# Attention jobs 4 to 7 beside the first half's feed-forward, and a different route for the second weight's decoding

## The chip, the core and the metric

The kernel is one program on one core of a Trainium2 chip. The metric is the device time of one execution in microseconds; lower is better. The profile is one profiled execution of the same program. A core has five engines that run side by side, each taking its own instructions strictly in order: TensorE (PE, matrix products; PEld are its weight loads), VectorE (DVE), ScalarE (ACT), GpSimd (POOL) and SyncE (SP), which here issues nearly all DMA transfers. Two more things matter below. A DMA that has to wait for its source or its buffer makes every later DMA of the same issuing engine wait too. And matrix results live in PSUM, here in eight tiles, which only VectorE and ScalarE read in this kernel.

## What is computed

Attention with a decay bias over 8 batches of 8 heads, 576 positions and 64 dimensions per head, and then a feed-forward layer on the result:

```python
scores = scale * np.matmul(q, k.transpose(0, 1, 3, 2))
s_pos = np.maximum(s, 0.0)
cum = np.cumsum(s_pos, axis=-1)
bias = -(cum[:, :, :, None] - cum[:, :, None, :])
scores = np.where(causal, -1000000000.0, scores + np.minimum(bias, 0.0))
scores = scores - np.max(scores, axis=-1, keepdims=True)
attn = np.exp(scores)
attn = attn / (np.sum(attn, axis=-1, keepdims=True) + 1e-09)
attn_out = np.matmul(attn, v)
x = attn_out.transpose(0, 2, 1, 3).reshape(B * S, H * D)   # 4608 x 512
h = x @ w_in                                               # 4608 x 2048
g = np.where(h >= 1, h, np.where(h <= -1, 0.0, (h + 1) ** 2 / 4))
return g @ w_out                                           # 4608 x 512
```

The two weights arrive as 64-bit floats, seen by the kernel as pairs of 32-bit integers.

## The kernel before

**Attention.** A job is one pair of heads of one batch, and one half of the queries: `hf` 0 has the first 320 positions, `hf` 1 the last 256. There are 64 jobs; the four pairs of batch 0 in the first half are jobs 0 to 3, the same pairs in the second half jobs 4 to 7. A job runs through eight slots (`att_slot`, from L468): its queries and keys are split into a leading and a remaining part (`att_prep`, L320), score blocks are computed on PE (L385, L386), VectorE adds the mask and takes the minimum (L391), ScalarE takes the exponential and its row sums (L402), the weights are scaled and split in two 16-bit halves on GpSimd, ScalarE and VectorE (`weights_t`, L408 to L429), and a transposing DMA (L430) brings them into the layout that the product with the values needs. Slot 7 of a job computes the product for the job before it (`att_out`, L437), and its result is scaled and split into the feed-forward's input `x` (L459, L460). `x0_0` is that input for batch 0, first half; `x0_1` the one for the second half.

**Feed-forward.** For each batch and half, 16 tiles `h` of 128 hidden units (12 matmuls each, L502) are turned into `g` by ScalarE (L514, L528), VectorE (L517, L518) and GpSimd (L529), and 16 times 12 matmuls with the second weight sum up four tiles `y` (L541). Two `h` tiles fit in PSUM.

**The weights.** Each weight is cut in 16 chunks of 128 x 512 values. For each, `decode` (L187) forms the 32-bit value from the two integers: ScalarE writes the absolute value of the high word (L193), VectorE clamps it from below and keeps the row maximum (L194), shifts (L195) and puts sign and low bits back (L201, or L203 and L204); in every second chunk ScalarE first prepares the low bits (L200). When all peaks of a weight (of half of it for `w2`) are known, `scale` (L206) makes one power of two from them: a maximum over the partitions through PE (`column_max`, L105; the tile is `row_wi`, `row_wo`), then spread to all partitions (`spread`, L113; `col_wi`, `col_wo`). `split` (L219) then writes the high 16-bit half on ScalarE (L222) and the low one, for 8 chunks of `w2` on VectorE (L230), for the other 8 on ScalarE and GpSimd (L227, L228). The first weight's names are `wir`, `WI`; the second's `wor` (as loaded), `WO` (decoded, then split).

**The order of the work.** First 1: jobs 0 to 3, with two chunks of the first weight decoded per pair of slots (L574 to L580), then its `scale` and `split`. Then the loop over `j` (L606): steps 0 to 15 each compute one `h` tile of batch 0, first half, and run two tasks of the second weight, of which there are 32; steps 16 to 31 compute the `y` matmuls of that half. Attention goes on from step `ATT_FROM` = 12, two slots a step, so 40 slots up to step 31. From step 32 on, each step does one slot and half an `h` or `y` step. The order in which instructions stand on each engine is not that of the source: a scheduler with priorities (`tc.high_priority`) sets it when the program is built.

**Buffers.** A chunk of the second weight is loaded into a buffer with tag `x0` or `x1`, two of each, in turn. The input `x` of the feed-forward uses the same tags, and `x0_0` occupies one of the `x0` while its `h` tiles are computed. So the even chunks have one buffer and the odd ones two. `load(c + 2)` (L596) follows `decode(c)`. Queries, keys and the scaled values (`vb`, L349) have a single buffer each, so that a job's preparation waits until the job before is through with them.

## Time and profile before

| | |
|---|---|
| median of 3 runs | 1178.55 us (1178.08 to 1179.56) |
| the profiled execution's own time | 1180.32 us |
| its span, first to last instruction | 1178.5 us |
| PE busy | 1013.1 us, 86% of the span |
| VectorE busy | 892.5 us, 76% |
| ScalarE busy | 746.2 us, 63% |
| GpSimd busy | 693.4 us, 59% |
| mean granted PE clock | 0.961 |

A row of a windows view gives a stretch of the span in us, and for each engine its busy time and number of instructions, then the granted PE clock, the busy share of the DMA engines and their GB/s. A row of a view by lines gives line, engine, operation, output and inputs, shapes and count, then busy time, mean ns of one, and after the second bar the idle time that stood ahead of these instructions with what ended it. A row of a timeline or of the chain gives the start in us, the duration in us, and the instruction. A row of the waits gives who waited for whom: us in total, times, longest.

### The profile page before, as it was taken

How to read it: one execution, taken by the hardware profiler on the slowest of the kernel's cores; microseconds unless marked ns; L12 is line 12 of the kernel's file. 1: busy time of each engine (PE TensorE's matmuls, PEld its weight loads, DVE VectorE, ACT ScalarE, POOL GpSimd, SP SyncE). 2: the span in 40 equal slices, each digit the busy share in tenths (PEclk: the TensorE clock that was granted, in tenths of full speed). 3: DMA queues.
4: the chain of work that ended last, by engine and by line, in shares of the span. 5: the costliest groups of instructions: out<-in, count | busy, mean ns of one | idle time of the engine just before them, and what ended most of it. 6: DMA issues, size and time to landing. Idle time of an engine off the chain costs nothing.

```text
span 1178.5 us, 25143 instructions
## 1 busy us (share of the span) xinstructions
PE 1013.1 (86%) x8470; PEld 780.1 (66%) x8470; DVE 892.5 (76%) x2403; ACT 746.2 (63%) x1719; POOL 693.4 (59%) x1169
## 2 busy tenths in 40 slices
PE   0234697599998999899999999899999999899998
PEld 0122364478776877687768877677777767687787
DVE  7878987778777877778777877787777767787633
ACT  4656587467757775677657775667566665677533
POOL 3865248676546765566556654766557554676522
PEclk9997898689999999999998999999999999899999
DMA  8895326667538763676539763876457643767300
GB/s 245 208 197 134 121 66 153 153 139 159 139 77 189 155 156 84 132 164 150 134 78 174 158 142 76 185 143 154 101 124 159 133 118 84 159 136 158 80 25 19
DMA packets 343082, 158.04 MB, mean 134 GB/s; under 512 B 291113, under 2 KB 324265, under 8 KB 342953
## 3 DMA queue, kind: packets, MB, share of 16 engines
q1 hardware_dynamic: 333248, 146.50, 56.3%
q10 hardware_dynamic: 9704, 9.93, 2.7%
q8 instruction: 67, 1.10, 0.4%
q14 instruction: 63, 0.51, 0.1%
HBM read 75.33 MB, written 9.73 MB: 72 GB/s over the span
## 4 chain that ended last, share of the span: by engine, by line
PE 57%; DVE 12%; POOL 11%; DMA 11%; issue 6%; ACT 4%; SPq 0%; DVEq 0%; ACTq 0%; POOLq 0%
PE y L541 24%; PE h L502 23%; DMA pt<-pb 4%; PE px L448 4%; DMA vt<-vb 3%; PE s L385 3%; PE s L386 2%; POOL pb L423 2%; POOL pb L426 2%; DVE pb L429 2%; DMA wor<-in_moe_w_out_dram 1%; POOL vb L351 1%; DVE p L391 1%; DMA wir<-in_moe_w_in_dram 1%; POOL pb L425 1%
## 5 line engine op out<-in xcount | busy, mean ns | idle before, releaser
L502 PE MATMUL h<-x,WI 128*128 128x256 f16 (+1 forms) x3072 | 452.9, 292 | 24.8 <-DVE u L518 16.9
L541 PE MATMUL y<-g,WO 128*128 128x256 f16 (+1 forms) x3072 | 452.3, 290 | 16.5 <-POOL g L529 9.9
L502 PEld LDWEIGHTS <-WI 128*128 128x128 f16 x3072 | 291.9, 100 | 119.6 <-issue 30.4
L541 PEld LDWEIGHTS <-WO 128*128 128x128 f16 x3072 | 287.6, 99 | 107.0 <-issue 24.5
L529 POOL TENSOR_TENSOR g<-u,g 128x320 f16<-128x320 f32 (+1 forms) x256 | 202.4, 790 | 205.8 <-ACT g L528 200.1
L514 ACT ACTIVATE u<-h,ub,us 128x320 f32<-128x320 f32 (+1 forms) x256 | 149.4, 584 | 168.2 <-PE h L502 160.1
L402 ACT ACTIVATE p<-p,mn 64x64 f32<-64x64 f32 (+4 forms) x320 | 178.7, 559 | 114.9 <-DVE mn L391 96.5
L517 DVE SCALAR_TENSOR_TENSOR h<-h,ws,u 128x320 f32<-128x320 f32 (+1 forms) x256 | 133.1, 520 | 107.6 <-ACT u L514 107.1
L423 POOL TENSOR_SCALAR pb<-p,rs 64x128 f16<-64x128 f32 (+4 forms) x160 | 112.8, 705 | 154.0 <-DVE rs L419 114.8
L385 PE MATMUL s<-K,Q 128*128 128x288 f32 (+4 forms) x384 | 150.6, 395 | 41.8 <-DVE mn L391 31.9
L429 DVE SCALAR_TENSOR_TENSOR pb<-p,rs,pb 64x128 f16<-64x128 f32 (+4 forms) x160 | 131.9, 825 | 51.0 <-POOL pb L423 50.3
L426 POOL TENSOR_TENSOR pb<-p,pb 64x128 f16<-64x128 f32 (+4 forms) x160 | 165.0, 1032 | 9.1
L391 DVE CUSTOM_DVE_ANT_0 p<-s,mask 64x64 f32<-64x64 f32 (+4 forms) x320 | 134.7, 422 | 46.8 <-PE s L386 40.7
L518 DVE SCALAR_TENSOR_TENSOR u<-u,r,h 128x320 f32<-128x320 f32 (+1 forms) x256 | 130.2, 510 | 8.7 <-DVE h L517 0.9
L424 ACT ACTIVATE p<-p,rs 64x64 f32<-64x64 f32 (+4 forms) x160 | 89.3, 559 | 66.2 <-DVE rs L419 63.4
L386 PE MATMUL s<-K,Q 68*128 68x288 f32 (+4 forms) x384 | 121.9, 319 | 8.9 <-ACT p L424 4.7
L448 PE MATMUL px<-pt,vt 128*64 128x256 f16 (+3 forms) x1536 | 92.1, 269 | 29.5 <-DMA pt<-pb 18.3
L385 PEld LDWEIGHTS s<-K,Q 128*128 128x128 f32 (+1 forms) x384 | 74.4, 194 | 64.4 <-DVE mn L391 40.4
L528 ACT CAST g<-u 128x320 f16<-128x320 f32 (+1 forms) x256 | 108.0, 422 | 13.9 <-DVE u L518 13.9
L448 PEld LDWEIGHTS <-vt 128*64 128x64 f16 x1536 | 76.8, 118 | 53.8 <-issue 27.3
L425 POOL TENSOR_SCALAR pb<-p 64x128 f16<-64x128 f32 (+4 forms) x160 | 91.2, 571 | 5.5 <-ACT p L424 2.4
L386 PEld LDWEIGHTS s<-K,Q 68*128 68x128 f32 (+1 forms) x384 | 75.6, 197 | 11.6 <-ACT p L424 5.1
(116 smaller groups left out, 961.9 us busy)
## 6 DMA issues: line engine op xcount, KB each, us to landing
rk<-in_k_dram SPq DMA_DIRECT2D x64, 288.0 KB
rq<-in_q_dram SPq DMA_DIRECT2D x64, 160.0 KB
rk<-in_k_dram SPq DMA_DIRECT2D x64, 160.0 KB
v<-in_v_dram SPq DMA_DIRECT2D x32, 288.0 KB
wir<-in_moe_w_in_dram SPq DMA_DIRECT2D x16, 512.0 KB
rq<-in_q_dram SPq DMA_DIRECT2D x64, 128.0 KB
wor<-in_moe_w_out_dram SPq DMA_DIRECT2D x16, 512.0 KB
out_dram<-o ACTq DMA_DIRECT2D x32, 160.0 KB
```

What stands on the lines that cost most here:

```text
L385: T.matmul(sc[:R, :c1 - c0], Q1[:, hd, qo:qo + R], K1[:, hd, c0:c1], start=True, stop=False)
L386: T.matmul(sc[:R, :c1 - c0], Q2[:KC, hd, qo:qo + R], K2[:KC, hd, c0:c1], start=False, stop=True)
L391: ttr[0] = V.tensor_tensor_reduce(out=Pt[:R, c0:c1], in0=sc[:R, :c1 - c0], in1=mask[:R, mo:mo + c1 - c0], scale=1.0, scalar=3.0e38 if mn i ...
L402: A.activation(Pt[:R, :W], Pt[:R, :W], AF.Exp, bias=m2[:R], scale=-1.0, accum_out=sums[n, i][:R, hd:hd + 1])
L423: G.tensor_scalar(his[0], pv, rs[:R, :1], 1.0, ALU.mult, ALU.mult)
L426: G.tensor_tensor(los[1], pw, his[1], ALU.subtract)
L429: V.scalar_tensor_tensor(los[0], pv, rs[:R, :1], his[0], ALU.mult, ALU.subtract)
L448: T.matmul(px[hd * D:(hd + 1) * D, lo:N], VT[:, vl * NB + j, hd * D:(hd + 1) * D], PT[:, 4 * j + 2 * hd + pl, lo:], start=(m == 0), stop=( ...
L502: T.matmul(h[:, :N], WI[4 * kt + ft // 4][:, wl, ft % 4 * P:(ft % 4 + 1) * P], x[:, kt, xl], start=(n == 0), stop=(n == 3 * NKT - 1),)
L514: first = A.activation(u, h[:, :N], AF.Relu, bias=ubi[b], scale=usc[b]).ins
L529: G.tensor_tensor(g[:, 1], u, g[:, 0], ALU.subtract)
L541: T.matmul(ys[b, hf, m][:, :N], WO[8 * (m // 2) + ft // 2][:, wl, c0:c0 + P], g[:, gl], start=(ft == 0 and n == 0), stop=(ft == NFT - 1 an ...
```

## The change

It has three parts.

1. **Attention in steps 0 to 31.** `ATT_FROM` goes. Steps 0 to 31 now do one slot each, and two in every fourth step: again 40 slots, so that step 32 finds the same job.
2. **The second weight's decoding and splitting.** The clamp moves from VectorE to GpSimd (new L195) and no longer delivers a row maximum. Instead, a new pass of ScalarE over the decoded chunk writes absolute values into the chunk's load buffer and adds them up by row (new L210). `scale` uses the largest row sum as the bound and leaves out two small VectorE steps. All 16 low halves now go over ScalarE and GpSimd (`POOL_LO`). The loads' buffers are now the two of tag `raw`, which the prefix sums used at the program's start, and those of `x0`, in the order raw, x0, raw; three chunks are loaded ahead, and `load(c + 3)` follows `decode(c)`.
3. **The value scales of batch 0** (`batch_scales_v(0)`, a second maximum over the partitions through PE) move from ahead of job 0 into its slot 6.

```diff
-POOL_LO = {'wi': (2, 3, 7, 11, 15), 'wo': range(1, 16, 2)}
+POOL_LO = {'wi': (2, 3, 7, 11, 15), 'wo': range(16)}
-ATT_FROM = 12
...
             A.activation(w, hw.bitcast(F32), AF.Abs)
-            V.tensor_scalar(w, w, LEAST_HI, LEAST_HI, ALU.max, ALU.max, accum_out=self.peak[:, c:c + 1])
+            if self.sums:
+                G.tensor_scalar(w, w, LEAST_HI, LEAST_HI, ALU.max, ALU.max)
+            else:
+                V.tensor_scalar(w, w, LEAST_HI, LEAST_HI, ALU.max, ALU.max, accum_out=self.peak[:, c:c + 1])
...
+            if self.sums:
+                A.activation(
+                    raw[:, :NC // 2].rearrange("p n t -> p (n t)").bitcast(F32), w, AF.Abs,
+                    accum_out=self.peak[:, c:c + 1],
+                )
...
-        WO[WO_LAG:], WO, (("x0", 2), ("x1", 2)), 2,
+        WO[WO_LAG:], WO, ((ap, "raw", 2), (gp, "x0", 2), (ap, "raw", 2)), 2, True,
...
     def batch_start(b):
         batch_v(b)
-        batch_scales_v(b)
+        if b:
+            batch_scales_v(b)
...
             att_slot(j, k)
+            if j == 0 and k == 6:
+                batch_scales_v(0)
...
-    for c in range(2):
+    for c in range(3):
         w2.load(c, w1.bound[0])
...
                 w2.decode(c)
-                w2.load(c + 2)
+                w2.load(c + 3)
...
-        for _ in range(1 if j >= 2 * NFT else 2 if j >= ATT_FROM else 0):
+        for _ in range(1 if j >= 2 * NFT else 1 + (j % 4 == 3)):
             att_slot(t // 8, t % 8)
```

How the instructions then stand, at three places. In a row, the name left of the arrow is what is written; a name's first numbers are its own (`s0_1_0_0` is a score block of pair 0, query block 1, head 0; `wor15` is chunk 15 of the second weight), its last number only counts tiles.

On PE, at the start of the program, before: the maximum of the value scales (`row_m0`, `col_m0`) stands ahead of job 0's score blocks.

```order
L108 MATMUL row_m0_183<-ident_77,mt0_180 1x128
L118 LDWEIGHTS ones_82
L118 MATMUL col_m0_189<-t16_m0_187,ones_82 128x1
L385 MATMUL s0_0_0_0_227<-K1_90,Q1_89 64x64
L386 MATMUL s0_0_0_0_227<-K2_92,Q2_91 64x64
```

And of the change, from its fifth row on:

```order
L395 MATMUL s0_1_0_0_250<-K1_90,Q1_89 128x192
L396 MATMUL s0_1_0_0_250<-K2_92,Q2_91 128x192
L395 MATMUL s0_1_1_0_262<-K1_90,Q1_89 128x192
L396 MATMUL s0_1_1_0_262<-K2_92,Q2_91 128x192
L395 MATMUL s0_2_0_0_286<-K1_90,Q1_89 128x320
L396 MATMUL s0_2_0_0_286<-K2_92,Q2_91 128x320
L107 MATMUL row_m0_297<-ident_77,mt0_294 1x128
L117 LDWEIGHTS ones_82
L117 MATMUL col_m0_303<-t16_m0_301,ones_82 128x1
L395 MATMUL s0_2_1_0_312<-K1_90,Q1_89 128x320
```

Five of job 0's six score blocks now come first; the sixth still stands behind the maximum.

On ScalarE, while the second weight is decoded beside the `h` tiles, before: absolute values of chunks 2, 5 and 7 (`wor2`, `wor5`, `wor7`), low bits of chunk 2, and the two steps of each `h` tile (`u`, `g`).

```order
L193 ACTIVATE WO4_128<-wor2_883 128x512
L200 ACTIVATE wor2_883<-wor2_883,floor_bias_75 128x512
L193 ACTIVATE WO7_131<-wor5_922 128x512
L514 ACTIVATE u0_0_2_970<-h0_0_2_957,ub0_809,us0_805 128x320
L528 CAST g0_0_0_905<-u0_0_1_937 128x320
L193 ACTIVATE WO9_133<-wor7_955 128x512
```

And of the change, a little later in the same work:

```order
L210 ACTIVATE wor1_817,peak_wo_145<-WO3_127 128x512
L525 ACTIVATE u0_0_4_1112<-h0_0_4_1098,ub0_809,us0_805 128x320
L539 CAST g0_0_0_917<-u0_0_3_1063 128x320
L525 ACTIVATE u0_0_5_1144<-h0_0_5_1131,ub0_809,us0_805 128x320
L539 CAST g0_0_4_1111<-u0_0_4_1112 128x320
L193 ACTIVATE WO6_130<-wor4_902 128x512
L210 ACTIVATE wor3_894,peak_wo_145<-WO5_129 128x512
L203 ACTIVATE wor4_902<-wor4_902,floor_bias_75 128x512
```

Each chunk now passes ScalarE once more (L210), and that pass writes into the chunk's load buffer.

On SyncE's queue, where the last chunks of the second weight are loaded, before: the loads of the weight end ahead of the transposes of job 4 (`pt0_1`).

```order
L185 DMA wor10_1130<-in_moe_w_out_dram 128x2x512
L185 DMA wor12_1164<-in_moe_w_out_dram 128x2x512
L185 DMA wor14_1197<-in_moe_w_out_dram 128x2x512
L430 DMA_TRANSPOSE pt0_1_1322<-pb0_3_1323 128x16x128
L317 DMA rq2_1_1505<-in_q_dram 64x2x256 x2
L317 DMA rk2_1_1506<-in_k_dram 64x2x576 x2
L430 DMA_TRANSPOSE pt0_1_1322<-pb0_4_1414 128x20x128
```

And of the change:

```order
L185 DMA wor12_1254<-in_moe_w_out_dram 128x2x512
L185 DMA wor14_1313<-in_moe_w_out_dram 128x2x512
L327 DMA rq2_1_1293<-in_q_dram 64x2x256 x2
L327 DMA rk2_1_1294<-in_k_dram 64x2x576 x2
L185 DMA wor15_1350<-in_moe_w_out_dram 128x2x512
L440 DMA_TRANSPOSE pt0_1_1009<-pb0_4_1156 128x20x128
```

The queries and keys of job 6 (`rq2_1`, `rk2_1`) now come ahead of the last chunk's load, and job 4's second transpose stands behind that load.

More of the change, by code (lines that the diff above doesn't have):

```diff
@@ L165, in attention_ffn, with __init__ @@
     class Weights:
-        def __init__(self, name, src, held, out, tags, groups):
-            self.size = NW // groups
+        def __init__(self, name, src, held, out, tags, groups, sums):
+            self.size, self.sums = NW // groups, sums
             self.name, self.src, self.held, self.out, self.tags = name, src, held, out, tags
@@ L176, in load @@
             if c < NW:
-                tag, bufs = self.tags[c % len(self.tags)]
-                self.raw[c] = gp.tile([P, NC, 2], I32, tag=tag, bufs=bufs, name=f"{self.name}r{c}")
+                pool, tag, bufs = self.tags[c % len(self.tags)]
+                self.raw[c] = pool.tile([P, NC, 2], I32, tag=tag, bufs=bufs, name=f"{self.name}r{c}")
                 if after is not None:
@@ L210, in scale @@
             top = column_max(t, f"{self.name}{g}")
-            b = top.bitcast(I32)
-            V.tensor_scalar(b, b, 3, -0x40000000, ALU.logical_shift_left, ALU.bitwise_xor)
-            V.tensor_scalar(b, b, 0x7FFFFFFF, None, ALU.bitwise_and)
+            if not self.sums:
+                b = top.bitcast(I32)
+                V.tensor_scalar(b, b, 3, -0x40000000, ALU.logical_shift_left, ALU.bitwise_xor)
+                V.tensor_scalar(b, b, 0x7FFFFFFF, None, ALU.bitwise_and)
             pow2floor(top, top, least)
@@ L233, in attention_ffn @@
         "wi", lambda c: w_in[c // 4 * P:(c // 4 + 1) * P, c % 4 * NC:(c % 4 + 1) * NC, :],
-        WO, WI, (("g", G_BUFS),), 1,
+        WO, WI, ((gp, "g", G_BUFS),), 1, False,
     )
```

## The prediction

> **What bounds the kernel now.** I read the table of windows first, cut where the program's stages meet: the first weight and jobs 0 to 3 (to 91 us), the `h` tiles of batch 0's first half with the second weight's decoding (to 161), then attention jobs 4 to 7 with the `y` matmuls, to the output of job 4 (194), of job 6 (224) and of job 7 (235), then the rest.
>
> ```profile
> 0.00:91.00 91.00, 21.27 (x106) 14.82 (x106) 71.19 (x199) 49.26 (x103) 56.37 (x97) 1.00 0.87 214
> 91.00:161.00 70.00, 43.74 (x264) 27.55 (x265) 62.77 (x135) 47.06 (x78) 28.03 (x26) 0.85 0.40 122
> 161.00:194.00 33.00, 27.26 (x189) 18.07 (x187) 26.81 (x62) 26.89 (x50) 23.15 (x25) 0.95 0.41 95
> 194.00:224.00 30.00, 16.88 (x112) 12.18 (x110) 22.71 (x69) 14.87 (x31) 19.25 (x25) 0.72 0.62 145
> 224.00:235.00 11.00, 6.54 (x48) 5.20 (x48) 7.86 (x26) 6.77 (x21) 8.66 (x17) 0.62 0.85 179
> 235.00:700.00 465.00, 445.90 (x3850) 348.73 (x3849) 362.75 (x1004) 310.96 (x753) 291.31 (x523) 0.98 0.65 140
> 700.00:1100.00 400.00, 377.51 (x3259) 292.96 (x3257) 305.75 (x845) 261.37 (x625) 241.16 (x427) 0.97 0.60 130
> ```
>
> From 235 us on PE is busy 95% of the time, and the change leaves that work as it is. What it can win lies before: PE works only 115.7 of 235 us. In the second stage VectorE is the full engine (62.77 of 70), GpSimd the empty one (28.03). In the fourth, no engine is over 76%: it is a chain. Next, the waits and the lines of these stages:
>
> ```profile
> POOL g L529 <- ACT g L528: 32.2, 14, 4.7
> PE h L502 <- DVE u L518: 16.9, 8, 8.0
> ACT WO L193 <- DMA wor<-in_moe_w_out_dram: 11.7, 12, 2.3
> ```
>
> ```profile
> L194 DVE TENSOR_SCALAR_CACHE_REDUCE WO<-WO 128x512 f32<-128x512 f32 x15 | 10.1, 677 | 3.6 <-ACT WO L193 3.6
> L195 DVE TENSOR_SCALAR WO<-WO 128x512 int32<-128x512 int32 x14 | 9.8, 703 | 0.0
> L230 DVE SCALAR_TENSOR_TENSOR WO<-WO,r_wo,WO 128x512 f16<-128x512 f32 x4 | 3.7, 924 | 0.6 <-ACT WO L222 0.6
> L203 DVE SCALAR_TENSOR_TENSOR WO<-wor,WO 128x512 int32<-128x512 int32 x8 | 6.4, 804 | 0.0
> L193 ACT ACTIVATE WO<-wor 128x512 f32<-128x512 f32 x15 | 9.9, 669 | 13.2 <-DMA wor<-in_moe_w_out_dram 11.7 <-POOL WI L228 1.5
> L228 POOL TENSOR_TENSOR WO<-WO,WO 128x512 f16<-128x512 f32 x2 | 2.3, 1158 | 2.3 <-ACT WO L227 2.3
> ```
>
> PE waits for VectorE's `u` (16.9 us), and ScalarE waits for chunks to land (11.7 us). The one buffer of the even chunks shows in the timeline: L201 is the last reader of such a chunk, and the chain holds the next load right behind it.
>
> ```profile
> 107.54 1.64 DVE L201 SCALAR_TENSOR_TENSOR WO<-wor,WO 128x512 int32<-128x512 int32 x1
> 126.00 0.68 DVE L201 SCALAR_TENSOR_TENSOR WO<-wor,WO 128x512 int32<-128x512 int32 x1
> 136.18 1.27 DVE L201 SCALAR_TENSOR_TENSOR WO<-wor,WO 128x512 int32<-128x512 int32 x1
> 166.81 0.69 DVE L201 SCALAR_TENSOR_TENSOR WO<-wor,WO 128x512 int32<-128x512 int32 x1
> ```
>
> Two loads of the chain, start and duration:
>
> ```profile
> 110.77 4.79 DMA wor<-in_moe_w_out_dram
> 126.74 4.64 DMA wor<-in_moe_w_out_dram
> ```
>
> The first and the last are 59.3 us apart, for seven turns of that buffer: 8.5 us each.
>
> **The first stage: value scales behind job 0's scores.** Rows of three timelines tell how it starts and ends, first GpSimd's.
>
> ```profile
> 14.51 1.53 POOL L340 TENSOR_TENSOR K<-rk,K 64x640 fp32r<-64x640 f32 x1 [9.40 <-ACT K L335]
> 22.99 1.16 POOL L351 TENSOR_SCALAR vb<-v,rc 128x576 f16<-128x576 f32 x1 [6.96 <-DVE rc L258]
> ```
>
> PE's:
>
> ```profile
> 22.63 0.37 PE L108 MATMUL row_m<-ident,mt 128*1 128x128 f32 x1 [22.63 <-DVE mt L262]
> 25.73 0.32 PE L385 MATMUL s<-K,Q 128*64 128x64 f32 x1
> 85.35 1.65 PE L448 MATMUL px<-pt,vt 128*64 128x320 f16 x18 [5.96 <-DMA pt<-pb]
> 86.93 0.37 PE L108 MATMUL row_wi<-ident,t_wi 128*1 128x128 f32 x1
> ```
>
> And VectorE's last step on the first weight's peaks:
>
> ```profile
> 71.87 0.15 DVE L209 TENSOR_REDUCE t_wi<-peak_wi 128x1 f32<-128x16 f32 x1
> ```
>
> Job 0's operands are ready at 16.04 (14.51 + 1.53), its first score runs at 25.73 because PE's queue has `row_m` first. So the head start is 9.7 us at most. Little of it may last: the value preparation (22.99) still waits for the same reciprocal, job 0's sixth score block still waits for the maximum, and job 1 needs job 0's Q and K buffers. But the stage ends with attention, not with the weight: peaks are complete at 71.87, and `row_wi` stands behind job 2's output on PE until 86.93. Bounds: 0 (transfers take 0.87 of the stage already) and 9.7. I take **3 us gained**, nearer to the lower end, since VectorE's 71.19 busy us and the transfers leave little air.
>
> **The second stage: decoding beside the `h` tiles and job 4.** Up to the 16th `h` tile, VectorE loses 15 clamps (10.2 us by L194), 4 low halves (3.7 by L230) and the decoding of three chunks, which now comes later (3 shifts and some 5 passes, about 6 us by L195 and L203). It takes over part of job 4, from the order a scaling pass, a Q remainder and twelve half rows of mask and minimum. Their prices:
>
> ```profile
> L391 DVE CUSTOM_DVE_ANT_0 p<-s,mask 128x448 f32<-128x448 f32 (+4 forms) x28 | 12.5, 455 | 5.0 <-PE s L386 3.5 <-POOL pb L426 1.1
> L429 DVE SCALAR_TENSOR_TENSOR pb<-p,rs,pb 128x512 f16<-128x512 f32 (+4 forms) x13 | 13.9, 1068 | 2.6 <-POOL pb L423 2.5
> L402 ACT ACTIVATION_READ_ACCUMULATOR p<-p,mn 128x1 f32 (+1 forms) x28 | 5.3, 188 | 0.0
> L227 ACT ACTIVATE WO<-WO,r_wo 128x512 f32<-128x512 f32 x8 | 5.7, 717 | 0.1
> L225 POOL TENSOR_SCALAR WO<-WO,r_wi 128x512 f32<-128x512 f32 x5 | 7.1, 1427 | 6.9 <-ACT WI L222 6.9
> ```
>
> GpSimd's timeline, two passes of a tile with one input, and ScalarE's, the first absolute values of the second weight:
>
> ```profile
> 24.25 0.74 POOL L353 TENSOR_SCALAR v<-v,rc 128x576 f32<-128x576 f32 x1
> 43.15 4.09 POOL L353 TENSOR_SCALAR v<-v,rc 128x576 f32<-128x576 f32 x1
> ...
> 101.27 1.22 ACT L193 ACTIVATE WO<-wor 128x512 f32<-128x512 f32 x2
> ```
>
> The six masked blocks cost 2.7 us, the scaling pass 1.1, the rest about 2: VectorE goes from 62.8 to 49. No row shows the clamp on GpSimd. Its nearest are one-input passes of a tile: 0.74 us at 24.25, 1.43 on average for L225, 4.09 at worst. I take 1.0, near the undisturbed end, because VectorE is less full then. Fourteen in this stage are 14 us, 4 low halves (4.6 by L228) leave it, job 4 brings some 6: GpSimd goes from 28 to 43. ScalarE gets 10 sum passes at 0.669 + 0.188 = 0.86 (8.6 us) and job 4's exponentials (3 at about 0.8), and sheds 10 splitting passes (7.2): 47 to 51.
>
> The page GPSIMD Engine Reference of the Trainium skill, section Engine selection, puts two-input passes on GpSimd at about half VectorE's speed and one-input passes at about line rate. Here the low half takes 1.16 us on GpSimd and 0.92 on VectorE; doubling 0.92 would add 0.7 us to each of the eight moved halves, 5.5 us in all, on an engine that has the room up to 194 us.
>
> So no engine fills 70 us any more, and the chunk's round decides: landing 4.8 us behind its release (110.77), absolute value 0.67, clamp 1.0, shift 0.70, one or two passes of 0.80 (1.2), sum pass 0.86. That is 9.2 us bare. In a round each engine also serves the other two chunks and some four `h` tiles, so on each of the four hops a chunk meets about 1 us of queue: 13 us per round of three chunks, an estimate. The `h` tiles stand in step with it: the 16th follows the 12th chunk, so four rounds, 52 us, after the first absolute value at 101.3. The stage ends at 154 instead of 161: 63 us for 70, **7 gained**, less than VectorE's 14.
>
> **The third and fourth stage.** The third keeps its sums (ScalarE: five sum passes in, four splits out) and now holds the jobs 4 and 5 with `y` matmuls between them. But job 4's second transpose stands in SyncE's queue behind the load of chunk 15, which waits for a sum pass on ScalarE behind job 6's preparation. I let it take 29 us at 26.9 of ScalarE work, **4 gained**. The fourth stage receives what was put off: by the order, 22 splits on ScalarE (22 x 0.72 = 15.8 on top of 14.9, less overlap: 29) and 8 more low halves on GpSimd (9.3 on top of 19.3: 29). It was a chain of 30 us with room; now two engines need 29 each, in turn with the chain: 35 us, **5 lost**. What hid these splits before was the wait of the `h` tiles for VectorE. The fifth stage keeps its order.
>
> **Sum.** 3 + 7 + 4 - 5 = 9 us gained, carried to the end since all behind is PE's. Against the profiled execution: 1178.5 span + 1.8 around it = 1180.3, less 9 is 1171.3. That execution was 1.8 above the median of the runs, so I predict **1169.5 us** there. Later rows of the order differ by small swaps, for which I allow 3 us either way.
>
> **Rivals.**
>
> *The round through GpSimd becomes the bound, and the kernel slower.* Place: second and third stage. If the clamp runs near L225's 1.43 or L353's 4.09 while VectorE streams, and stands behind `g` tiles, a round takes 17 us: 5.3 rounds x 4 us = 21 lost against the forecast, 1190; half of that, at 15 us, is 1180. It decides from a round of 14.7 (9 / 5.3 above 13). For it: the one row of 4.09, and three load buffers held longer than before. Against it: the same tile passed in 0.74, and VectorE has 14 us less to do. GPSIMD Engine Reference of the Trainium skill (section Key points) has GpSimd share its memory interface with VectorE when that reads two inputs; the 4.09 fits, and L201 to L204 are such passes.
>
> *VectorE was all that held it.* Then the second stage shrinks by VectorE's 14 and the fourth loses nothing, because its splits fit into the chain's gaps: 3 + 14 + 4 = 21, so 1157.5. For it: 16.9 us of PE waits on `u`. Against it: the round above.
>
> *Nothing comes of it.* The head start is eaten by transfers (0.87) and what the second and third stage gain (11), the fourth gives back in full on ScalarE: 1178.5.
>
> **Chances.** A measurement of this kernel tells about 0.2%, 2.4 us, from no change. Forecast, anything from 3 to 16 us gained: 0.53. VectorE alone: 0.14. Nothing: 0.13. The round: 0.20. So faster 0.67, same 0.13, slower 0.20. The range, 1156 to 1184, takes in the second and third case and the round up to about 15.7 us; what is left out is the longer rounds and sums of all lucky ends. The forecast's own range is 1162.5 to 1175.5.
>
> **What would show it.** First score at about 16 us, `row_wi` at about 84. L201's successors for chunks of one buffer 13 us apart; clamps near 1.0; VectorE below 55 us up to the 16th `h` tile, that tile some 10 us earlier. Job 4's output about 14 us earlier, job 6's about 9: if the lead does not shrink between them, the fourth stage's term is wrong. Wrong altogether if the busy time of PE behind 235 us changes, or if SyncE's queue holds attention's loads for long behind a chunk.

## The result and the profile after

| | before | changed |
|---|---|---|
| median of 4 runs | 1178.32 us (1176.67 to 1179.56) | 1190.12 us (1186.90 to 1200.72) |
| profiled execution, its span | 1180.32, 1178.5 us | 1200.72, 1198.9 us |
| ratio to before | | 1.0107 (95%: 1.0080 to 1.0134) |

The change makes the kernel 12 us slower. The prediction had 9 us faster. The profiled execution of the changed kernel is the longest of its four; a second trace (experiment 5) is of one of 1187.78 us, and both are read here. One profiled execution of an experiment (the value scales alone) ran at a granted clock of 0.752 and took 1378.89 us; its trace isn't used, its times are those of the other runs.

The table of windows of the changed kernel, cut at the 16th `u` (159), and at the outputs of jobs 4 (181.1), 5 (201.8), 6 (223.2) and 7 (238.0); the last row goes from job 8's output to the 64th.

```profile
90.00:159.00 69.00, 40.81 (x228) 25.02 (x228) 55.38 (x108) 52.87 (x104) 56.30 (x44) 0.84 0.48 132
159.00:181.10 22.10, 10.92 (x67) 7.23 (x66) 19.60 (x29) 18.86 (x36) 21.02 (x20) 0.65 0.54 129
181.10:201.80 20.70, 18.46 (x137) 12.68 (x136) 12.71 (x32) 14.56 (x29) 13.94 (x16) 0.92 0.41 77
201.80:223.20 21.40, 17.07 (x134) 11.34 (x133) 15.96 (x40) 13.54 (x26) 18.16 (x21) 1.00 0.54 112
223.20:238.00 14.80, 6.44 (x53) 5.04 (x50) 9.30 (x34) 8.45 (x24) 12.91 (x21) 0.69 0.75 175
252.10:1147.35 895.25, 844.47 (x7269) 657.14 (x7268) 673.11 (x1852) 574.29 (x1377) 536.45 (x944) 0.98 0.61 131
```

The same last stretch before:

```profile
246.80:1127.05 880.25, 839.59 (x7267) 653.10 (x7267) 675.19 (x1854) 576.12 (x1380) 537.61 (x946) 0.98 0.61 133
```

VectorE has become lighter up to the 16th `u`: 55.4 us, for 62.8 before and 49 in the forecast's sum. But now GpSimd is the full engine: 56.3 of 69 us and then 21.0 of 22.1. TensorE's timeline says what came of it. First the outputs of jobs 4, 6, 7 and 8 before, then in the changed kernel (start, duration; a bracket gives the idle time of the engine ahead of the row and what ended it):

```profile
192.12 1.51 PE L448 MATMUL px<-pt,vt 128*64 128x256 f16 x30
220.11 2.77 PE L448 MATMUL px<-pt,vt 128*64 128x256 f16 x30
231.91 2.77 PE L448 MATMUL px<-pt,vt 128*64 128x256 f16 x30 [2.04 <-DVE Q L337]
245.84 0.94 PE L448 MATMUL px<-pt,vt 128*64 128x320 f16 x18
```

```profile
179.66 1.49 PE L458 MATMUL px<-pt,vt 128*64 128x256 f16 x18
221.73 1.51 PE L458 MATMUL px<-pt,vt 128*64 128x256 f16 x30
235.19 2.77 PE L458 MATMUL px<-pt,vt 128*64 128x256 f16 x30 [4.85 <-DMA pt<-pb]
251.32 0.80 PE L458 MATMUL px<-pt,vt 128*64 128x320 f16 x16
```

Job 4's output is 12.5 us earlier (forecast: about 14), and by job 6's the whole lead is gone; job 8's is 5.3 us late. In the second trace these are 14.3 early, 1.4 early, and 3.1 late. The rest of the loss lies behind: 895.2 us for 880.3 in this execution, 884.4 in the second, at the same granted clock of 0.98 as before; TensorE's busy time there, which was to stay, is 844.5 us for 839.6. On GpSimd, the lines between 100 and 200 us of the changed kernel show the full engine's load: the clamp, and for comparison a multiplication of the same tile.

```profile
L195 POOL TENSOR_SCALAR WO<-WO 128x512 f32<-128x512 f32 x16 | 33.8, 2115 | 5.7 <-ACT WO L193 5.7
L235 POOL TENSOR_SCALAR WO<-WO,r_wi 128x512 f32<-128x512 f32 x4 | 2.8, 694 | 0.0
```

The clamp takes 2.1 us on average, where the prediction took 1.0: 33.8 us instead of 16, three times the multiplication in these rows.

The last chunk shows how this reaches the second half's scale. Rows of four timelines of the changed kernel, first ScalarE's, then SyncE's queue, then GpSimd's and ScalarE's again, and TensorE's:

```profile
169.38 1.14 ACT L345 CAST K<-rk 128x1152 fp32r<-128x1152 f32 x1
170.42 0.62 ACT L210 ACTIVATE wor<-WO 128x512 f32<-128x512 f32 x1
...
175.94 0.65 ACT L193 ACTIVATE WO<-wor 128x512 f32<-128x512 f32 x1
...
187.08 0.63 ACT L210 ACTIVATE wor<-WO 128x512 f32<-128x512 f32 x1 [1.39 <-DVE WO L207]
```

```profile
171.16 0.38 SPq L185 DMA_DIRECT2D wor<-in_moe_w_out_dram  x1
171.64 3.90 SPq L440 DMA_TRANSPOSE pt<-pb  x1
```

```profile
179.81 1.16 POOL L238 TENSOR_TENSOR WO<-WO,WO 128x512 f16<-128x512 f32 x1
180.94 1.92 POOL L195 TENSOR_SCALAR WO<-WO 128x512 f32<-128x512 f32 x1
```

```profile
189.84 0.27 PE L107 MATMUL row_wo<-ident,t_wo 128*1 128x128 f32 x1
```

Chunk 15's load goes out at 171.16, right behind the sum pass at 170.42, which stood behind job 6's `K` on ScalarE. Its absolute value is ready at 176.6, but GpSimd, which has steps of the jobs and low halves ahead of it and is idle for only 0.3 us in between, takes the clamp only at 180.94. The sum pass comes at 187.08 and the second half's scale (`row_wo`) at 189.84. Before, it came 23 us earlier:

```profile
166.84 0.27 PE L108 MATMUL row_wo<-ident,t_wo 128*1 128x128 f32 x1 [0.52 <-DVE t_wo L209]
```

### The profile page after: what moved, and what is told of

It reads as the page before. It is cut to its first block, busy times and chain, and to the rows that moved or that the text cites. A ratio compares the mean times of both kernels' runs of the same rounds, so it can differ in the third digit from the quotient of the medians.

```text
span 1198.9 us, 25145 instructions
## 1 busy us (share of the span) xinstructions
PE 1016.6 (85%) x8470; PEld 782.1 (65%) x8470; DVE 887.6 (74%) x2360; ACT 759.1 (63%) x1759; POOL 733.0 (61%) x1193
## 4 chain that ended last, share of the span: by engine, by line
PE 50%; DVE 11%; POOL 11%; DMA 10%; issue 6%; ACT 5%; ACTq 0%; DVEq 0%; POOLq 0%
PE y L552 22%; PE h L513 21%; DMA pt<-pb 5%; PE px L458 4%; POOL pb L433 3%; DMA vt<-vb 3%; DVE pb L439 3%; POOL pb L436 2%; PE s L396 2%; PE s L395 2%; POOL g L540 1%; DMA out_dram<-o 1%; ACT p L412 1%; DVE p L401 1%; DMA wor<-in_moe_w_out_dram 1%
## 5 line engine op out<-in xcount | busy, mean ns | idle before, releaser
L433 POOL TENSOR_SCALAR pb<-p,rs 64x128 f16<-64x128 f32 (+4 forms) x160 | 115.5, 722 | 157.6 <-DVE rs L429 113.2
L395 PE MATMUL s<-K,Q 128*128 128x288 f32 (+4 forms) x384 | 149.0, 391 | 61.0 <-DVE mn L401 37.3
L439 DVE SCALAR_TENSOR_TENSOR pb<-p,rs,pb 64x128 f16<-64x128 f32 (+4 forms) x160 | 137.9, 862 | 50.8 <-POOL pb L433 50.6
L458 PE MATMUL px<-pt,vt 128*64 128x256 f16 (+3 forms) x1536 | 96.5, 276 | 45.4 <-DMA pt<-pb 34.0
L458 PEld LDWEIGHTS <-vt 128*64 128x64 f16 x1536 | 80.4, 121 | 69.6 <-issue 38.8
L435 POOL TENSOR_SCALAR pb<-p 64x128 f16<-64x128 f32 (+4 forms) x160 | 88.6, 554 | 4.4 <-ACT p L434 0.9
```

The lines of the kernel that those rows point to most:

```text
L395: T.matmul(sc[:R, :c1 - c0], Q1[:, hd, qo:qo + R], K1[:, hd, c0:c1], start=True, stop=False)
L433: G.tensor_scalar(his[0], pv, rs[:R, :1], 1.0, ALU.mult, ALU.mult)
L439: V.scalar_tensor_tensor(los[0], pv, rs[:R, :1], his[0], ALU.mult, ALU.subtract)
L458: T.matmul(px[hd * D:(hd + 1) * D, lo:N], VT[:, vl * NB + j, hd * D:(hd + 1) * D], PT[:, 4 * j + 2 * hd + pl, lo:], start=(m == 0), stop=( ...
```

## The experiments

Three theories were set against each other. A: the price of the clamp on GpSimd. B: the spread attention stands in the decoding's way. C: the start matters little, and the small differences of order behind job 8 decide. All times stand beside runs of the kernel before on the same chip, and the ratio is to those: their median was 1179.86 us for experiments 1 to 4, 1178.47 for 5 to 8, 1177.91 for 9 to 11 and 1181.30 for 12.

| kernel | median us | ratio to before (95%) | 2nd half's scale at | job 4 out | job 7 out | job 8 out | job 8 to 64th |
|---|---|---|---|---|---|---|---|
| before | 1178.32 | | 166.8 | 193.6 | 234.7 | 246.8 | 880.3 |
| changed, first trace | 1190.12 | 1.0107 (1.0080 to 1.0134) | 189.8 | 181.2 | 238.0 | 252.1 | 895.2 |
| changed, second trace | 1190.53 | 1.0100 (1.0065 to 1.0134) | 188.1 | 179.4 | 236.1 | 249.9 | 884.4 |
| 1 clamp on VectorE | 1170.63 | 0.9924 (0.9899 to 0.9949) | 174.1 | 174.6 | 225.2 | 238.9 | 881.0 |
| 2 spread alone | 1171.10 | 0.9935 (0.9902 to 0.9968) | 174.1 | 174.8 | 224.4 | 237.5 | 879.0 |
| 3 route alone | 1187.49 | 1.0064 (1.0042 to 1.0086) | 172.6 | 202.8 | 245.8 | 259.1 | 875.6 |
| 4 value scales alone | 1178.31 | 0.9989 (0.9970 to 1.0007) | | | | | |
| 6 light pass | 1174.13 | 0.9960 (0.9941 to 0.9979) | 179.9 | 181.6 | 230.6 | 243.6 | 874.8 |
| 7 one maximum | 1189.93 | 1.0093 (1.0064 to 1.0123) | 191.6 | 183.6 | 239.4 | 252.8 | 885.6 |
| 8 spread and buffers | 1175.34 | 0.9979 (0.9960 to 0.9998) | 173.2 | 173.6 | 226.4 | 239.3 | 884.6 |
| 9 route, VectorE clamp, no spread | 1178.81 | 1.0015 (0.9999 to 1.0031) | 166.2 | 195.0 | 239.6 | 251.8 | 873.6 |
| 10 GpSimd scales, VectorE clamp | 1180.22 | 1.0014 (0.9998 to 1.0030) | 174.1 | 176.4 | 230.6 | 244.4 | 882.6 |
| 11 odd low halves | 1185.65 | 1.0069 (1.0048 to 1.0090) | 185.9 | 176.7 | 235.9 | 249.0 | 884.5 |
| 12 late clamps on VectorE | 1177.68 | 0.9983 (0.9964 to 1.0002) | 179.4 | 176.5 | 227.6 | 238.6 | 882.2 |

The last five columns are us of each kernel's trace: the scale's `row_wo` is a start, the outputs are ends (start plus duration of the last row of that job in TensorE's timeline).

**1. Clamp on VectorE.**

```diff
-                G.tensor_scalar(w, w, LEAST_HI, LEAST_HI, ALU.max, ALU.max)
+                V.tensor_scalar(w, w, LEAST_HI, LEAST_HI, ALU.max, ALU.max)
```

> The changed kernel with the clamp back on VectorE; the sum passes on ScalarE, the 16 low halves on GpSimd, the load buffers and the spread attention stay. Theory A, the clamp's price: in the changed kernel the clamp took 2.1 us on GpSimd, 16 times, and GpSimd was busy 21.0 of the 22.1 us ahead of job 4's output. Back on VectorE (about 0.7 us each) GpSimd is at least 10 us freer there, the second half's scale of the second weight (its maximum through TensorE, at 189.8 us in the changed kernel, 166.8 before) comes by 175, job 7's output by 229 (238.0 in the changed kernel, 234.7 before), and the time is 1172 to 1179. Theory B, the spread attention stands in the way on ScalarE and in SyncE's queue whatever the clamp costs: the scale stays later than 183, job 7's output at 234 or later, time 1184 to 1191. Theory C, the start matters little, and the order of the rest (behind job 8's output) decides: whatever the start does, the stretch from job 8's output to the end differs from before by over 5 us.

One line turns 1.0100 into 0.9924, and the kernel beats both; it is even below the 1172 to 1179 of theory A. VectorE's line of that kernel for the clamp, between 100 and 200 us, and the table of windows to the outputs of jobs 4, 5 and 6:

```profile
L195 DVE TENSOR_SCALAR WO<-WO 128x512 f32<-128x512 f32 x16 | 9.4, 590 | 5.6 <-ACT WO L193 5.5
```

```profile
90.00:174.60 84.60, 49.74 (x294) 31.60 (x295) 72.07 (x154) 70.50 (x139) 44.90 (x43) 0.84 0.48 130
174.60:191.00 16.40, 13.26 (x111) 9.45 (x110) 12.47 (x30) 13.92 (x26) 16.01 (x19) 0.99 0.63 126
191.00:208.70 17.70, 15.28 (x126) 10.60 (x124) 14.35 (x35) 13.76 (x25) 17.24 (x21) 1.00 0.70 152
```

The clamp costs VectorE 0.59 us on average, GpSimd 2.12. The 16th `u` is ready at 167.5 here, 8.5 us later than in the changed kernel and 3.0 later than before, and the kernel is still faster than both. So the 16th `u`, by which the prediction measured the second stage, isn't what the time depends on. B's signs are absent, though the spread stays in this kernel, and so is C's (881.0 us behind job 8's output, 880.3 before). Of the 20 us or so between this kernel and the changed one, the traces show 11.0 to 13.2 ahead of job 8's output. The rest lies behind it, where executions scatter (experiment 5), and no run shows what of it is the clamp's.

**2. The spread alone**, in the kernel before.

```diff
-        for _ in range(1 if j >= 2 * NFT else 2 if j >= ATT_FROM else 0):
+        for _ in range(1 if j >= 2 * NFT else 1 + (j % 4 == 3)):
```

> The kernel before with the attention slots of jobs 4 to 7 spread over steps 0 to 31, and nothing else. Theory A (clamp's price): no clamp on GpSimd, so no great loss; VectorE, the full engine of the second stage, now also carries job 4's blocks there, so the 16th tile u comes about 6 us later than the 164.0 before, but job 4's output comes earlier than 193.6; time within 6 us of before. Theory B (the spread attention itself delays the weight): the second half's scale comes 10 us or more later than 166.8, job 7's output at 240 or later, time 1184 to 1192. Theory C (order of the rest): the stretch from job 8's output to the end differs by over 5 us.

The gain is that of the first experiment, with nothing of the weight's route changed. TensorE's timeline, outputs of jobs 4 and 7:

```profile
174.34 0.45 PE L448 MATMUL px<-pt,vt 128*64 128x192 f16 x9
221.66 2.77 PE L448 MATMUL px<-pt,vt 128*64 128x256 f16 x30 [4.38 <-DMA pt<-pb]
```

Theory A had "within 6 us of before", which was too little: the spread gains 0.65%, 7.7 us. VectorE is busy 80.3 of the 84.8 us up to job 4's output, fuller than before, and the time doesn't suffer from it: the 16th `u` is 2.8 us later than before, the second half's scale is 7.3 us later than before, and job 7's output 10.3 earlier.

**3 and 9. The new route alone**, with the clamp on GpSimd and on VectorE. Both have attention from step 12 on and the value scales in their old place; the second has the edit of experiment 1 as well.

```diff
-        for _ in range(1 if j >= 2 * NFT else 1 + (j % 4 == 3)):
+        for _ in range(1 if j >= 2 * NFT else 2 if j >= 12 else 0):
...
-        if b:
-            batch_scales_v(b)
+        batch_scales_v(b)
...
-            if j == 0 and k == 6:
-                batch_scales_v(0)
```

> The changed kernel with attention again from step 12 on and the value scales again ahead of job 0: the new route of the second weight alone. Theory A: clamps at 2 us each fill GpSimd, but without job 4 beside them it has the room (34 of some 70 us, 14 for the g tiles, low halves behind); the 16th tile u comes at 156 to 160, job 4's output at 186 to 192, and the time is 1173 to 1180. If the clamp's 2.1 us decides by itself, without job 4, the 16th u is not earlier than 164 and the time is 1184 or more. Theory B: without the spread, the second half's scale is at most at 170 and the time is below 1178. Theory C: the stretch from job 8's output to the end differs from before by over 5 us.

> The new route with the clamp on VectorE, attention again from step 12 and the value scales again ahead of job 0: the sum passes, the 16 low halves on ScalarE and GpSimd and the new buffers alone. Theory V, as the prediction had it: what the route takes off VectorE (the low halves, and nothing else now) and the earlier loads are worth a few us even without the spread: 1171 to 1175. Theory S, the spread carries the whole gain, because jobs 4 to 7 are a chain that only starts too late: job 7's output within 3 us of the 234.7 before, time 1176 to 1182.

The first is 0.6% slower than before, outside the times that A and B had forecast, and in time what the expectation gave to the clamp deciding by itself (1184 or more): the clamp on GpSimd costs even without job 4 beside it. But it doesn't do so by the `h` tiles, as the expectation had put it. Its 16th `u` is there at 148.6, 15.9 us earlier than before, and job 4's output 9.2 us later; by which waits isn't worked out here. TensorE's timeline of that kernel, jobs 4 and 7:

```profile
201.27 1.51 PE L458 MATMUL px<-pt,vt 128*64 128x256 f16 x30 [1.62 <-DMA pt<-pb]
243.01 2.77 PE L458 MATMUL px<-pt,vt 128*64 128x256 f16 x30 [1.26 <-DMA pt<-pb]
```

The second, 1.0015, can't be told from before: in the time that is theory S, and V's gain is absent. S's sign in the trace is missed: job 7's output, at 239.6, is 4.9 us later than before (3 were allowed), and the stretch behind job 8's is 6.7 us shorter in this execution, so the even time is made of a later start and a shorter rest. With 1 and 2 the four kernels make a square: without GpSimd's clamp, the spread is worth 0.65 to 0.9% and the route nothing; with it, the spread is worth nothing (1.0064 without, 1.0100 and 1.0107 with). The moved value scales are in some corners and not in others, which by experiment 4 is about 1 us.

**4. The value scales alone**, moved into job 0's slot 6.

```diff
-        batch_scales_v(b)
+        if b:
+            batch_scales_v(b)
...
+            if j == 0 and k == 6:
+                batch_scales_v(0)
```

> The kernel before with only the value scales of batch 0 moved into slot 6 of job 0. The changed kernel's third output came 4.0 us earlier than before (83.0 against 87.0), and its first h matmul 1.5 us earlier. Theory A and B: the same here, 1 to 4 us earlier at the start, and the time is 1174.5 to 1178. Theory C: the rest's order, which this edit alters too (about 200 small differences on TensorE), moves the stretch from job 8's output to the end by over 5 us either way.

0.9989 (0.9970 to 1.0007): about 1 us, somewhere between 0.8 lost and 3.5 gained. The stretch that theory C spoke of can't be read without the trace.

**5. The changed kernel once more.**

> The changed kernel once more, unaltered, for a second trace of it. Its profiled execution took 1200.72 us, its other runs 1186.9 to 1192.88; between job 8's output and the end it was 15 us longer than before, with TensorE waiting 22.3 us for transposed weights behind 250 us (9.0 before). If that belongs to the order of the rest, it comes again here: job 8's output at about 252, and 10 to 15 us lost behind it. If it belonged to that one execution, job 8's output is again at about 252 and the stretch behind it within 4 us of before: 1184 to 1190.

Job 8's output is at 249.9 (252.1), the rest 4.1 us longer than before (15.0 in the first trace). That is nearer to the second forecast: 4.1 us where 4 were allowed, 1190.53 where 1190 was the most, job 8's output 2 us early. So most of the 15 us belonged to that one execution, and some 4 us are lost behind job 8 here too. TensorE's waits from 250 us on, before, in the first and in the second trace:

```profile
PE px L448 <- DMA pt<-pb: 9.0, 10, 2.2
```

```profile
PE px L458 <- DMA pt<-pb: 22.3, 14, 2.8
```

```profile
PE px L458 <- DMA pt<-pb: 20.7, 15, 2.4
```

The wait for transposed weights looks like the cause, but the kernel of the first experiment has it too (20.8 us) and spends 881.0 us there, as before. Over all traces but the first one of the changed kernel that stretch is 873.6 to 885.6 us, whatever the start did. Theory C has a share of up to 7 us either way, then. Of the 12 us lost only 3.1 to 5.3 stand ahead of job 8's output in the two traces; but by experiments 1, 6 and 12 the sign goes with the clamp.

**6 and 7. What in the clamp is dear.** In the first, VectorE clamps, and GpSimd passes over the same tile with two multiplications by 1.0. In the second, GpSimd clamps with one maximum in place of two.

```diff
-                G.tensor_scalar(w, w, LEAST_HI, LEAST_HI, ALU.max, ALU.max)
+                V.tensor_scalar(w, w, LEAST_HI, LEAST_HI, ALU.max, ALU.max)
+                G.tensor_scalar(w, w, 1.0, 1.0, ALU.mult, ALU.mult)
```

```diff
-                G.tensor_scalar(w, w, LEAST_HI, LEAST_HI, ALU.max, ALU.max)
+                G.tensor_scalar(w, w, 1.0, LEAST_HI, ALU.mult, ALU.max)
```

> The kernel with the clamp on VectorE, and in GpSimd's place a pass over the same tile that multiplies by 1.0 twice, between the clamp and the shift: the detour over GpSimd stays, only the operation is another. Multiplying passes of this form took 0.70 us in the changed kernel, the clamp 1.9 to 2.4. Theory A1, the price of the maximum: the pass takes 0.7 to 0.9, second half's scale at 174 to 179, time 1170 to 1176. Theory A2, the detour itself (a chunk waits for its turn on GpSimd between attention and g tiles): scale later than 183, time above 1181.

> The changed kernel with the clamp on GpSimd as a multiplication by 1.0 and one maximum, in place of two maxima. Theory A1 (each maximum costs GpSimd about 0.6 us more than a multiplication: 1.91 for two maxima, 0.70 for two multiplications): 1.3 us undisturbed, 10 us less on GpSimd over the 16, time between the two, 1176 to 1185. If any pass with a maximum takes 1.9 us, nothing changes: 1186 to 1191.

GpSimd's line for these passes, between 100 and 200 us, first with two multiplications, then with one maximum:

```profile
L196 POOL TENSOR_SCALAR WO<-WO 128x512 f32<-128x512 f32 x16 | 11.6, 730 | 9.5 <-DVE WO L195 9.5
```

```profile
L195 POOL TENSOR_SCALAR WO<-WO 128x512 f32<-128x512 f32 x16 | 33.3, 2080 | 7.5 <-ACT WO L193 7.4
```

The first is A1 in its price and its time (1174.13), with the scale 0.9 us later than A1's latest (179.9). Against the first experiment the detour over GpSimd still costs some 4 us, at the edge of the two intervals, and job 4's output is as late as in the changed kernel (181.6); but the jobs behind make up part of it: job 8's is 8.5 us ahead of the changed kernel's and 4.7 behind that of the first experiment. The second falls: one maximum costs what two cost, so A1's "0.6 us for each maximum" is wrong. In the changed kernel and in this one a pass with a maximum takes 1.91 to 2.39 us, in the other one two multiplications 0.61 to 1.06. The least is 1.91, so that at most 0.5 us of such a pass can be put down to the work of others beside it. The page GPSIMD Engine Reference of the Trainium skill, section Engine selection, puts one-input passes on GpSimd at about line rate, in a row that names add, multiply and maximum together. The multiplications come near it (on average 0.73 us beside 0.59 for VectorE's clamp, at least 0.61 beside 0.41), the maximum doesn't (2.12, at least 1.91). Why isn't settled here.

**8. The spread, the value scales and the buffers**, without the new route.

```diff
-POOL_LO = {'wi': (2, 3, 7, 11, 15), 'wo': range(16)}
+POOL_LO = {'wi': (2, 3, 7, 11, 15), 'wo': range(1, 16, 2)}
...
-        WO[WO_LAG:], WO, ((ap, "raw", 2), (gp, "x0", 2), (ap, "raw", 2)), 2, True,
+        WO[WO_LAG:], WO, ((ap, "raw", 2), (gp, "x0", 2), (ap, "raw", 2)), 2, False,
```

> The changed kernel without the new route: clamp with row maximum on VectorE, low halves of the odd chunks on GpSimd, no sum passes; the spread attention, the moved value scales and the new load buffers with three chunks ahead stay. The spread alone gave 1171.1. If VectorE's load is what still holds the second stage, the buffers give nothing and the time is 1169 to 1173; if chunks that come earlier let the h tiles and the second weight's scale come earlier, 1164 to 1169. If the freed VectorE was worth anything with the clamp back (the kernel of the first experiment), this one is above its 1170.6.

1175.34, above both ranges: earlier loads buy nothing that shows, and beside the spread alone some 5 us are lost by the ratios (in the two traces 1.8 up to job 8 and 5.7 behind it, where executions scatter). The third forecast holds as it was put: with buffers and value scales in place, the route is worth 0.5% (0.9979 here, 0.9924 with it). But the spread alone has neither and is as fast, so the route there at best makes up for what the other two cost. The value scales alone cost nothing that shows (experiment 4); the buffers alone were not tried.

**10. The scaling ahead of the low halves on GpSimd**, clamp on VectorE (the edit of experiment 1 beside this one).

```diff
-POOL_SCALE = ('wi',)
+POOL_SCALE = ('wi', 'wo')
```

> The kernel with the clamp on VectorE (1170.6), and the scaling ahead of each low half of the second weight moved from ScalarE to GpSimd, as the first weight has it: a multiplication, which takes 0.6 to 0.7 us there. ScalarE loses 16 passes of 0.71 us (11.4 us of the 70.5 that it is busy in the 84.6 us ahead of job 4's output), GpSimd gains 16 of about 0.7 (45 of 84.6 before that). If ScalarE holds the decoding and the jobs there, job 7's output comes 2 to 6 us earlier than 225.2 and the time is 1164 to 1169; if the chain of the jobs holds it, nothing: 1169 to 1173.

Missed: 1180.22, 0.9% slower than the kernel of the first experiment. The table of windows of this kernel from job 4's output to job 5's:

```profile
176.40:192.30 15.90, 11.34 (x86) 7.82 (x85) 12.64 (x23) 7.71 (x15) 15.90 (x18) 0.89 0.63 128
```

GpSimd is busy 15.90 of 15.90 us there, ScalarE 7.71. The 45 of 84.6 us ahead of job 4's output, which the expectation leaned on, say nothing of the stretch behind it, where GpSimd had been 16.0 of 16.4 and 17.2 of 17.7 already.

**11. Low halves of the even chunks on VectorE**, clamp on GpSimd.

```diff
-POOL_LO = {'wi': (2, 3, 7, 11, 15), 'wo': range(16)}
+POOL_LO = {'wi': (2, 3, 7, 11, 15), 'wo': range(1, 16, 2)}
```

> The changed kernel, clamp on GpSimd, with only the odd chunks' low halves on ScalarE and GpSimd, the even ones on VectorE again. By the account of GpSimd's load, 8 x 1.2 = 9.6 us leave GpSimd and 8 x 0.71 = 5.7 leave ScalarE; but the clamps of the last chunks, which make the second half's scale late, stand ahead of most low halves. If any 10 us off GpSimd helps alike, 1178 to 1184; if the clamps ahead of the last chunks decide, 1184 to 1190.

1185.65, in the second range; some 4 us better than the changed kernel by the ratios, whose intervals overlap, with the scale still at 185.9: ten us off GpSimd, but behind the clamps, help less than those ahead.

**12. The clamps of chunks 8 to 15 on VectorE.**

```diff
-            if self.sums:
+            if self.sums and c >= 8:
+                V.tensor_scalar(w, w, LEAST_HI, LEAST_HI, ALU.max, ALU.max)
+            elif self.sums:
                 G.tensor_scalar(w, w, LEAST_HI, LEAST_HI, ALU.max, ALU.max)
```

> The changed kernel with the clamp of chunks 8 to 15 on VectorE and that of chunks 0 to 7 on GpSimd: half of the maxima's price stays, in the part where job 4 is only beginning. Theory L, the late chunks decide: GpSimd was busy 37.3 of the 40 us from 140 to 180 us in the changed kernel, the clamp of the last chunk waited there, and the second half's scale came at 189.8 us; with these eight off GpSimd the scale comes by 180, job 7's output by 230 (238.0 in the changed kernel, 225.2 with all clamps on VectorE), time 1172 to 1178. Theory H, each clamp costs alike: half of the 20 us between the changed kernel and the one with all clamps on VectorE comes back: 1179 to 1182, job 7's output at 231 to 233. If the first eight decide: 1185 to 1190.

The stretch from 140 to 180 us in the tables of windows, the changed kernel first, then this one:

```profile
140.00:180.00 40.00, 19.87 (x108) 12.62 (x109) 37.21 (x65) 32.84 (x66) 37.33 (x30) 0.76 0.53 144
```

```profile
140.00:180.00 40.00, 20.45 (x125) 12.75 (x125) 36.42 (x75) 32.50 (x64) 23.78 (x24) 0.79 0.51 133
```

GpSimd falls from 37.3 to 23.8 us, the scale comes at 179.4, job 7's output at 227.6, job 8's at 238.6, as in the first experiment. That is theory L in the trace. In the time, two thirds of the loss come back (0.9983, between 1.0100 and 0.9924): nearer to L, but by time alone H isn't excluded.

## Why the prediction was wrong

**The step that failed** is the clamp's price: "I take 1.0, near the undisturbed end, because VectorE is less full then." It measured 2.1 on average, and 1.91 at the least. The rows it was taken from (0.74, 1.43, 4.09 at worst) are multiplications. They are the nearest by engine, shape and number of inputs, but not by operation. With it fell the next sentence, GpSimd "from 28 to 43": it was 56.3 of 69 us. That it is this step the first experiment shows: with the clamp alone put back the ratio is 0.9924, 9.0 us below 1178.3, and the forecast was 9. Experiment 6 shows that it is the price and not the detour over GpSimd: with a pass of 0.73 us in the clamp's place, and the clamp on VectorE, the kernel is 4.7 us faster than before (0.9960), which the forecast's own range takes in. In the kernels with the spread the time follows the second half's scale, as far as the table goes: where it comes by 180 the ratio is 0.9924 to 0.9983 (1.0014 in experiment 10, whose GpSimd has other work), where it comes at 185.9 or later 1.0069 to 1.0107.

**But that the first experiment lands on the 9 is luck.** In it job 4's output is 19.0 us earlier where the terms made 14, and the fifth stage, which was to keep its order, loses 4.7. The terms were off and made up for each other:

*The first stage, 3 us.* Measured: about 1.5. The first score did come at 14.4 and `row_wi` at 82.96 (forecast 16 and 84). TensorE's timeline of the changed kernel shows where it went:

```profile
82.96 0.37 PE L107 MATMUL row_wi<-ident,t_wi 128*1 128x128 f32 x1
88.62 0.16 PE L117 MATMUL col_wi<-t_wi,ones 1*128 1x1 bf16 x1 [5.28 <-DVE t_wi L115]
```

And that of the kernel before, then of the spread alone, which doesn't have this edit:

```profile
90.11 0.16 PE L118 MATMUL col_wi<-t_wi,ones 1*128 1x1 bf16 x1 [2.81 <-DVE t_wi L116]
```

```profile
88.21 0.16 PE L118 MATMUL col_wi<-t_wi,ones 1*128 1x1 bf16 x1 [2.81 <-DVE t_wi L116]
```

The maximum is 4 us earlier, and its second step 1.5, since VectorE takes 5.3 instead of 2.8 us for the small work between. Without the edit that step came at 88.21 to 90.11 us in four traces (89.2 on average), with it at 86.36 to 88.62 in nine (87.7): half of the term, and in the time not told from nothing (experiment 4).

*The second stage, 7 us.* The 16th `u` was ready at 159.0 (154 forecast) for 164.5 before, 5.5 us gained, with VectorE at 55.4 us instead of 49. Yet by itself this buys nothing: the kernel with the earliest 16th `u` (148.6) is 0.6% slower than before, and one with a late one (167.5) is one of the two fastest. "PE waits for VectorE's `u` (16.9 us)" was read as the bound; in the first experiment PE waits 25.2 us for it between 90 and 240 us, where it waited 16.9 before. Up to 235 us PE has room. That it is the end of the chain of jobs, and not the last `h` tile, that hands over to the PE-bound rest is a reading of the table: jobs 7 and 8 come 8 to 10 us earlier in the two fastest kernels.

*The round.* 13 us per three chunks was too little with this clamp. ScalarE's timeline, absolute values of chunks 0 (the first of the two in its row), 3, 6, 9 and 12 (chunk 13 passes at 155.59, ahead of 12: behind its clamp VectorE takes L206 and L207, as for odd chunks only):

```profile
99.83 1.26 ACT L193 ACTIVATE WO<-wor 128x512 f32<-128x512 f32 x2
114.16 0.66 ACT L193 ACTIVATE WO<-wor 128x512 f32<-128x512 f32 x1
130.50 0.64 ACT L193 ACTIVATE WO<-wor 128x512 f32<-128x512 f32 x1
142.21 0.68 ACT L193 ACTIVATE WO<-wor 128x512 f32<-128x512 f32 x1 [1.23 <-DMA wor<-in_moe_w_out_dram]
158.65 0.67 ACT L193 ACTIVATE WO<-wor 128x512 f32<-128x512 f32 x1
```

To chunk 15 (175.94) that makes rounds of 14.3, 16.3, 11.7, 16.4 and 17.3 us, 15.2 on average (15.3 in the second trace), above the 14.7 from which the rival *the round through GpSimd* was to decide, and at the end its 17. So that rival had the mechanism and, at 1190, the time; its sum didn't give that time, since 15.2 us a round come to about 1181 by it. The forecast's 13 itself was sound for the price that it was given: from the first to the last absolute value it is 13.0 a round in experiment 6, with passes of 0.73 us. In experiment 3, with clamps of 2.0 us but without job 4 beside them, it is 13.0 too. So it was the clamps and job 4's steps together, in GpSimd's queue, that stretched it, and the last chunk above all.

*The third stage, 4 us, and the fourth, 5 lost.* Job 4's output came 12.5 to 14.3 us earlier, as summed (14). The fourth lost 12.8 in both traces instead of 5. The reason given was the count of splits, 29 us on each of two engines; they were busy 28.1 and 32.1 us, near it, but in 42.1 us. What filled the stage was TensorE, busy 35.5 of the 42.1 us between jobs 4 and 6 (16.9 of 30 in the fourth stage of before): of its `y` matmuls 26.6 us stand there, where it had been 2.0, and then it is busy only 6.4 of 14.8 us, when job 7 has no `y` left beside it. In the first experiment 20.0 us of `y` stand there as well, and the stage takes 34.1 us, 4.8 more than before. So some 5 us come without the clamp on GpSimd, the size that was forecast, and 8 with it. That the scale, 23 us late, holds the splits and these the `y` matmuls fits the trace, where TensorE waits five times for GpSimd's low halves, but these waits make up only 2.6 us. The wait in SyncE's queue behind chunk 15's load, named as a risk, was there (from 159.5 to 171.16 nothing was issued), but it is part of the late chunk.

*What really gains* is the spread itself (experiment 2). Jobs 4 to 7 are a chain of their own, and before it could not begin until step 12. It started earlier and lost nothing that counted, although VectorE became fuller by it: job 4's output came 18.8 us earlier and job 7's 10.3. The prediction costed the spread as load on the engines and never gave the earlier start a term.

*The rest, 3 us either way.* Between job 8's output and the 64th the kernels differ by up to 6.7 us from the 880.3 of before, and the changed kernel's first trace by 15.0. The edits alter small things of the order to the end; 3 us was too narrow. What made one execution lose 11 us more there than another of the same program stays open.

The kernels of experiments 1 and 2 beat both kernels. Between them no difference can be told (1170.63 and 1171.10 on the same chip); the second needs one line.

## What to carry to other kernels

Price a moved operation by a row of the same operation on the engine that it moves to; the same shape and engine with another operation was wrong by a factor of three here. Ask of each stage which event hands over to the bound work that follows, and cost only what moves that event: an engine at 95% ahead of it (VectorE in experiment 2) may have nobody waiting who matters. And read an engine's room from each stretch in which the moved work will stand, not from the stage as a whole.

## What the runs showed of the chip

- GpSimd, one pass over 128x512 in f32: with a maximum 1.91 to 2.39 us, whether one or two of its operations are maxima (means 2.08 and 2.12); with two multiplications 0.61 to 1.06, 0.73 on average. VectorE does the clamp in 0.59 on average.
- One program's executions lie apart by several microseconds: 1186.90 to 1194.88 us in seven of the changed kernel, and one at 1200.72; 1174.02 to 1183.45 in the 14 runs of the kernel before beside experiments 1 to 4.
